# A fused RWKV-6 and MLP kernel: own terms of two rounds summed on TensorE, loads issued in program order, round 1 transposed within round 0, and twelve low words kept in the tiles of h

## The chip, the cores and the metric

The kernel runs on one core of one Trainium2 chip. The metric is the device time of one execution in microseconds. A core has five engines with an instruction queue each: TensorE (PE in the profile; its weight loads are PEld), VectorE (DVE), ScalarE (ACT), GpSimd (POOL) and SyncE (SP). In this kernel SP and ACT also issue the DMAs (SPq and ACTq in the profile). An engine works through its own queue in order, and waits on semaphores for the others.

## What is computed

The reference, cut to what matters. The inputs r, k, v, w are 4 x 8 x 768 x 48 (batch, head, time, channel), all float32; the two weights are 384 x 1536 and 1536 x 384, in float64 when they come in (the kernel reads them as pairs of 32-bit words).

```python
for t in range(S):                                   # attention, per batch and head
    cur = einsum(u * k[t], v[t])                     # the "own term" of step t
    y[t] = einsum(r[t], state + cur)
    state = w[t][:, None] * state + einsum(k[t], v[t])
x = y as (B, S, H*D)                                 # 4 x 768 x 384
xn = (x - mean) / sqrt(var + 1e-06) * g_ln
out = x + maximum(xn @ w_ch1, 0) @ w_ch2
```

## The kernel before, in words

**Rounds and units.** The work is cut into 8 rounds (4 batches x 2 halves of 384 time steps), and a round into 2 units of 4 heads. Units are numbered 0 to 15, two to a round. For each unit four loads of 72 KB each bring in w, k and r (one DMA per head, `load`, L120) into `nat_w`, `nat_k`, `nat_r`, which are double: a unit's number mod 2 chooses the buffer. v is loaded by four DMAs (`load_v`), and a second copy `vx` of the odd heads with its two halves of partitions exchanged comes from memory by four DMAs more (`load_vx`).

**Attention.** `turned` transposes w, k, r of one pair of heads on TensorE (three transposes), and ACT copies the PSUM tile out to wT, kT, rT. There are two PSUM buffers for this (`ps_t`). Then follow six levels. In a level, `quads` makes 24 small products per unit on TensorE (a_ps), `grow` multiplies rT and kT in place by the decays on DVE, and `keep` puts the products under a mask into A on DVE. `quads` of a level reads what `grow` of the level before has written, and `grow` of the level may not overwrite it before `quads` has read it, so that TensorE and DVE take turns. The decays' products come from `totals`. Behind the last level come `ends` (transposes of kT into kn), `states` (kv on TensorE, the states s on DVE), `exchanged` (ACT), `outputs` (y on TensorE, x on DVE). The own term is `take` (two products and a sum of 128 x 576 on DVE or POOL, which read `nat_k` and `nat_r` and the broadcast `u_bc`) and `own_term` (the sum times v).

**MLP.** `mlp` is a generator with 24 steps of three large matmuls each: 12 for h (one PSUM tile of 384 columns each, ReLU on ACT) and 12 for the output (o_ps). `fill(until, tasks)` spreads the tasks of a level evenly among the MLP steps that are due by then. From round 1 on, each level (here: slot, six to a round) is one call of it.

**Weights.** The weights come as 24 parts of 128 x 384 values (384 KB each as raw words). `fetch` loads a part into one of four `raw` buffers, `begin` makes three ACT instructions of it (one to w_sb, two to `rest`, the low words) and then fetches the part four ahead, and `join` makes three DVE instructions that put both together. `rest` has four buffers, so `begin` of a part waits for `join` of the part four before it. `converted` sees that a step of the MLP comes after the joins of its parts.

**What sets the order.** `InOrder` (L39) wraps PE, ACT, DVE and POOL, so that their instructions stand in the queue in the order of the program. SP was not wrapped: a scheduler placed its DMAs. All records of wrapped engines have line L49, that of the wrapper, and are told apart by tiles.

**Round 0** (L609 to L677) is written out by hand: transposes of units 0 and 1, six levels with idle matmuls between (`warm`), half of unit 2's and 3's transposes, the outputs, the layer norm, and the first weight parts. With L677 the MLP of round 0 begins.

Of the kernel before, what the change touches and what calls it, by code (L numbers as in the profile page):

```python
# [52 lines left out]
def kernel(  # L53
# [13 lines left out]
    PE, ACT, DVE, POOL = (  # L67
        InOrder(tc, e) for e in (nc.tensor, nc.scalar, nc.vector, nc.gpsimd)
# [22 lines left out]
    assert D <= HP and U == 2 and S % RN == 0 and DM % P == 0 and DF % P == 0  # L91
# [6 lines left out]
    p6 = ctx.enter_context(tc.tile_pool(name="p6", bufs=6))  # L98
    ph = ctx.enter_context(tc.tile_pool(name="ph", bufs=12))
# [20 lines left out]
    def load(q, which="wkr", eng=SP):  # L120
        for nm in which:
            for j in range(NH):
                eng.dma_start(
                    out=nat[nm][q % 2][:, ts(j // 2, TT), j % 2, 0:D],
                    in_=steps({"w": w, "k": k, "r": r}[nm], q, j),
                )

    def load_v(q):
        vn[q] = p4.tile([P, NH, TT, D], F32, tag="v", name=f"v{q}")
        for j in range(NH):  # L130
            SP.dma_start(out=vn[q][:, j], in_=steps(v, q, j))  # L131

    def load_vx(q):

        vx[q] = p4.tile([P, NP, TT, D], F32, tag="vx", name=f"vx{q}")
        for pr in range(NP):
            src = steps(v, q, 2 * pr + 1)
            for i in range(2):
                SP.dma_start(out=vx[q][ds(C * (1 - i), C), pr], in_=src[ds(C * i, C)])


    load(0, "wk")
    load(0, "r", ACT)
    load(1, "wk")
    u_bc = const.tile([P, H, D], F32, name="u_bc")
    ACT.dma_start(
        out=u_bc,
        in_=bass.AP(tensor=u.tensor, offset=u.offset, ap=[[0, P], [D, H], [1, D]]),
    )
# [3 lines left out]
    nought = const.tile([P, P], F32, name="nought")  # L153
    DVE.memset(nought, 0.0)
    eps = const.tile([P, 1], F32, name="eps")
# [6 lines left out]

    ident = const.tile([P, P], F32, name="ident")
    make_identity(nc, ident)
# [43 lines left out]
    def fetch(n=1, eng=ACT):  # L208
# [8 lines left out]
    def begin():  # L217
        nonlocal begun
        i = begun
        if i < len(parts):  # L220
            words = raw.pop(i)
            lo, hi = words[:, :, 0].bitcast(U32), words[:, :, 1].bitcast(F32)
            rest[i] = p4.tile([P, WC], I32, tag="rest", name=f"rest{i}")
# [30 lines left out]
    def warm(n):  # L254

        ps = ps_m.tile([P, RN], F32, tag="m", name="idle")
        for _ in range(n):
            PE.matmul(ps[:, 0:P], nought, nought, start=True, stop=True)
# [53 lines left out]
    def own_sums(q):  # L312
        o = st[q]["own"] = p2.tile([P, NH, TT], F32, tag="own", name=f"own{q}")
# [3 lines left out]
            axis=AX.X, op=ALU.add,  # L317
        )
# [179 lines left out]
    def norm(rnd):  # L498
# [6 lines left out]
        for i in range(TT):  # L505
            xn = p3.tile([P, H, D], F32, tag="xn", name=f"xn{rnd}_{i}")
# [18 lines left out]
    def mlp(rnd):  # L525
# [13 lines left out]
        for i in range(TT):  # L539
            ps = ps_m.tile([P, H, D], F32, tag="m", name=f"o_ps{name}_{i}")  # L540
            for f in range(FC):
                converted(len(parts) - FC + f + 1)
                PE.matmul(
                    ps.rearrange("p h d -> p (h d)"), hs[f][:, ts(i, P)], w2_sb[:, f, :],
                    start=f == 0, stop=f == FC - 1,
                )
                if f % KC == KC - 1 and f < FC - 1:
                    yield
            o = p2.tile([P, H, D], F32, tag="o", name=f"o{name}_{i}")
            DVE.tensor_tensor(out=o, in0=ps, in1=x[:, i], op=ALU.add)  # L550
            SP.dma_start(
                out=out[b, ds(f0 * RN + i * P, P), :].rearrange("t (h d) -> t h d", d=D), in_=o
            )
# [42 lines left out]
    pairs = range(NP)  # L596

    def take(eng, q):

        own_products(q, eng)  # L600
        own_sums(q)

# [8 lines left out]
    fetch(4, SP)  # L611
# [3 lines left out]
    take(DVE, u0)  # L615
    quads(u0, 0)
    load(new[0])
    for q in (u0, u1):
        load_v(q)
        load_vx(q)  # L620
    warm(2)
    grow(u0, 0)
    for nm in "wrk":
        run(each(turned, [u1], nm, pairs))
        warm(1)
    totals(0, DVE)
# [154 lines left out]
```

## Time and profile before

| what | value |
|---|---|
| runs | 636.33, 640.31, 642.42 us (median 640.31) |
| profiled execution, its own time | 638.57 us |
| its span, first to last instruction | 636.8 us, so 1.8 us lie around it |
| PE / DVE / ACT / POOL busy | 576.8 / 293.7 / 202.0 / 80.2 us |
| mean granted TensorE clock | 0.957 |
| DMA | 36.83 MB, 123250 packets, 116896 of them under 512 B |

How to read it: "busy" sums the durations of instructions; matmuls are pipelined, so that the start of the next row says more than the length of one. In a row of the timeline stand its start, its length, engine and line, the operation, output<-input, shapes, the number of instructions merged, and in brackets how long the engine stood idle before it and what released it. An h step is 3 matmuls and stands as 6 records.

### The profile page before, as it was taken

The page shows a single profiled execution, that of the slowest core. Times are in us where ns is not written, and L with a number is a line of the kernel's source. Part 1 is how long each engine was busy: PE and PEld are TensorE (multiplying, and loading weights), DVE is VectorE, ACT ScalarE, POOL GpSimd, SP SyncE. Part 2 cuts the span into 40 slices and gives each one's busy share as a digit, 9 for nine tenths or more (in the row PEclk, how much of TensorE's full clock was granted, in tenths as well). Part 3 has the DMA queues.
Part 4 walks back from the last instruction along what each step waited for, and adds up shares of the span by engine and source line. Part 5 has one row for each costly group of instructions (what it writes and reads, how often), then busy time and mean ns, then how long its engine had stood idle before and what let it go on. Part 6 is the DMA issues. An engine that isn't in the chain of part 4 may idle for free.

```text
span 636.8 us, 19302 instructions
## 1 busy us (share of the span) xinstructions
PE 576.8 (91%) x8560; PEld 392.5 (62%) x8560; DVE 293.7 (46%) x700; ACT 202.0 (32%) x426; POOL 80.2 (13%) x109
## 2 busy tenths in 40 slices
PE   6990983758999999999999999999999999999997
PEld 6880752436666666666666766667666666666554
DVE  3991697467464626272445543634427261221000
ACT  2361565556124321342124311441242104311200
POOL 6000001051006000240006000700040000000000
PEclk8995688869899999999999999999999999999999
DMA  9755577340432223113302241202100000000000
GB/s 166 169 95 114 106 185 188 105 107 8 92 63 51 38 48 74 31 31 63 75 27 39 47 85 29 51 1 47 39 14 2 9 21 13 1 14 25 1 12 25
DMA packets 123250, 36.83 MB, mean 58 GB/s; under 512 B 116896, under 2 KB 120096, under 8 KB 123168
## 3 DMA queue, kind: packets, MB, share of 16 engines
q1 hardware_dynamic: 116544, 26.96, 20.9%
q10 hardware_dynamic: 6624, 8.65, 5.0%
q8 instruction: 67, 1.10, 0.7%
q14 instruction: 15, 0.12, 0.1%
HBM read 30.87 MB, written 4.72 MB: 56 GB/s over the span
## 4 chain that ended last, share of the span: by engine, by line
PE 83%; DVE 4%; SPq 4%; ACT 3%; issue 3%; DMA 2%; ACTq 1%; DVEq 0%
PE o_ps L49 29%; PE h_ps L49 28%; PE a_ps L49 11%; PE y L49 3%; PE r_ps L49 2%; PE k_ps L49 2%; PE kv L49 2%; PE kn_ps L49 2%; PE xT_ps L49 2%; PE w_ps L49 1%; ACT rest L49 1%; DVE w_sb L49 1%; PE idle L49 1%; SPq L131 1%; DMA nat_k<-in_k_dram 1%
## 5 line engine op out<-in xcount | busy, mean ns | idle before, releaser
L49 PE MATMUL h_ps<-xT,w_sb 128*128 128x384 f32 x576 | 200.9, 500 | 5.7 <-DVE w_sb L49 3.3
L49 PE MATMUL o_ps<-w_sb,h 128*128 128x384 f32 x576 | 197.6, 489 | 2.0 <-DVE w_sb L49 2.0
L49 PEld LDWEIGHTS h_ps<-xT,w_sb 128*128 128x128 f32 x576 | 108.9, 195 | 74.7 <-issue 4.7
L49 PEld LDWEIGHTS o_ps<-w_sb,h 128*128 128x128 f32 x576 | 105.0, 191 | 63.1 <-DVE w_sb L49 2.6
L49 PEld LDWEIGHTS a_ps<-rT,kT 48*64 48x64 f32 x4608 | 75.4, 137 | 16.1 <-issue 14.1
L49 PE MATMUL a_ps<-rT,kT 48*64 48x32 f32 x4608 | 80.5, 221 | 4.4 <-issue 4.1
L49 ACT ACTIVATE h<-h_ps 128x384 f32<-128x384 f32 x96 | 46.4, 490 | 120.1 <-PE h_ps L49 115.7
L49 DVE TENSOR_TENSOR o<-o_ps,x 128x384 f32<-128x384 f32 x24 | 13.4, 557 | 136.6 <-PE o_ps L49 136.6
L49 DVE COPY_PREDICATED A<-mask,a_ps 128x384 f32<-128x384 int8 x80 | 54.5, 751 | 0.0
L49 POOL TENSOR_TENSOR vo<-v,own 128x576 f32<-128x576 f32 x12 | 13.9, 1156 | 308.0 <-DVE own L49 308.0
L49 DVE TENSOR_TENSOR rT<-rT,tot 128x384 f32<-128x384 f32 x80 | 43.7, 555 | 11.5 <-PE a_ps L49 11.5
L49 DVE TENSOR_TENSOR kT<-kT,tot 128x384 f32<-128x384 f32 x80 | 44.3, 554 | 8.3 <-PE a_ps L49 7.5
L49 DVE SCALAR_TENSOR_TENSOR s<-s,decay,kv 128x48 f32<-128x48 f32 x160 | 29.4, 258 | 35.3 <-PE kv L49 35.3
L49 DVE TENSOR_TENSOR x<-y,vo 128x288 f32<-128x288 f32 x32 | 13.2, 452 | 60.0 <-PE y L49 60.0
L49 PE MATMUL k_ps<-ident,nat_k 128*128 128x128 f32 x96 | 16.7, 302 | 20.5 <-DMA nat_w<-in_w_dram 16.5
L49 ACT ACTIVATE xT<-xT_ps,g_sb 128x384 f32<-128x384 f32 x24 | 13.8, 580 | 64.8 <-PE xT_ps L49 64.7
L49 ACT ACTIVATE rest<-raw 128x384 int32<-128x384 uint32 (+1 forms) x48 | 28.5, 594 | 4.4 <-DVE w_sb L49 3.7
L49 ACT COPY kT<-k_ps 128x384 f32<-128x384 f32 x32 | 14.7, 479 | 46.8 <-PE k_ps L49 46.4
L49 ACT COPY rT<-r_ps 128x384 f32<-128x384 f32 x32 | 14.8, 480 | 45.9 <-PE r_ps L49 45.9
L49 PEld LDWEIGHTS k_ps<-ident,nat_k 128*128 128x128 f32 x96 | 12.6, 155 | 25.8 <-ACT wT L49 17.2
L49 POOL TENSOR_TENSOR rk<-nat_k,nat_r 128x576 f32<-128x576 f32 x12 | 17.0, 1416 | 85.2 <-DVE own L49 84.8
L49 PE MATMUL r_ps<-ident,nat_r 128*128 128x128 f32 x96 | 17.1, 307 | 11.7 <-ACT rT L49 7.4
(63 smaller groups left out, 577.8 us busy)
## 6 DMA issues: line engine op xcount, KB each, us to landing
raw<-in_moe_w_ch_dram ACTq DMA_DIRECT2D x20, 384.0 KB, 3.3
nat_w<-in_w_dram SPq DMA_DIRECT2D x64, 72.0 KB, 2.4
nat_k<-in_k_dram SPq DMA_DIRECT2D x64, 72.0 KB, 2.4
v<-in_v_dram SPq DMA_DIRECT2D x64, 72.0 KB, 2.7
out_dram<-o SPq DMA_DIRECT2D x24, 192.0 KB, 1.9
nat_r<-in_r_dram SPq DMA_DIRECT2D x56, 72.0 KB, 2.4
vx<-in_v_dram SPq DMA_DIRECT2D x64, 36.0 KB, 2.2
raw<-in_moe_w_ch_dram SPq DMA_DIRECT2D x4, 384.0 KB, 4.8
```

What stands on the lines that cost most here:

```text
L49: return lambda *args, **kw: self.tc.keep_in_program_order(f(*args, **kw))
L131: SP.dma_start(out=vn[q][:, j], in_=steps(v, q, j))
```

## The change

1. **SP in program order.** `SPO = InOrder(nc.sync)`. All loads of round 0, the loads for units 4 and 5 in round 1, and every fetch of a weight part are issued by it (the weight parts' loads were ACT's from the fifth part on). r of unit 1 moves from ACT's queue to SP's.
2. **Own terms of units 0 to 3 on TensorE** (`own_by_pe`): two DVE products of 128 x 384 per unit from rT and kT, six matmuls of two columns with a tile `sel` that holds u in the columns of the two heads of a pair, and one ACT copy of 12 columns. `u_bc` is loaded only in round 1.
3. **vx from vn**: two DMAs per unit, SBUF to SBUF, in place of four from memory.
4. **Round 1 turned within round 0**: all twelve groups of transposes of units 2 and 3 stand between levels 1 to 4, where three groups of unit 2 stood at levels 3 and 4.
5. **Low words in the tiles of h**: `rest` of parts 0 to 11 uses the twelve buffers of h, and begin of these waits for no join; parts 12 to 23 have four buffers. Five parts are begun within the levels of round 0 where one was; eight by the start of the MLP where five were.
6. **The order after round 0**: `UNTIL` sets the MLP steps due by each slot: 16 at the end of round 1 (13 before), 33 at the end of round 2 (28 before), 48 at slot 16, near the end of round 3, in both, and the same from there. Round 1 has 3, 3, 3, 4, 4, 4 joins in its six slots and 3, 3, 3, 3, 4, 0 begins (before: 3, 2, 2, 3, 3, 4, 4 of both, in seven). In round 2 the states of both old units come in slot 0, outputs and layer norm in slot 1, `take` of units 4 and 5 in slot 2. `totals` of rounds 0, 1 and 2 stand on DVE behind the first `grow`. In round 0's MLP the first two output tiles are summed side by side.
7. **Small**: idle matmuls read a broadcast column of zeros.

The core of the diff:

```diff
+    PE, ACT, DVE, POOL, SPO = (
+        InOrder(tc, e) for e in (nc.tensor, nc.scalar, nc.vector, nc.gpsimd, nc.sync)
...
+        for i in range(2):
+            eng.dma_start(
+                out=vx[q][ds(C * (1 - i), C)].rearrange("p r c d -> p r (c d)"),
+                in_=vn[q][ds(C * i, C)]
+                .rearrange("p (r j) c d -> p r j (c d)", j=2)[:, :, 1],
+            )
...
-    load(0, "wk")
+    load(0, "w", SPO)
     load(0, "r", ACT)
-    load(1, "wk")
-    u_bc = const.tile([P, H, D], F32, name="u_bc")
-    ACT.dma_start(
...
-    load(1, "r", ACT)
+    load(0, "k", SPO)
+    load(1, "wrk", SPO)
+
+    sel = const.tile([P, H // 2, 2], F32, name="sel")
+    POOL.memset(sel, 0.0)
+    for j in range(2):
+        ACT.dma_start(
+            out=sel[ds(HP * j, D), :, j], in_=u.rearrange("(r j) d -> j d r", j=2)[j]
+        )
...
+    held = [ph.tile([P, RN], F32, tag="h", name=f"held{i}") for i in range(FC)]
+    LOW = 4
+
+    def fetch(n=1, eng=SPO):
...
-        if i < len(parts):
+        if i < len(parts) and i - joined < (len(held) if i < len(held) + LOW else LOW):
...
+            if i < len(held):
+                rest[i] = held[i].bitcast(I32)
+            else:
+                rest[i] = low.tile([P, WC], I32, tag="rest", name=f"rest{i}")
...
+    def own_by_pe(q):
+        b, f, g = units[q]
+        a = st[q]
+        ps = ps_t.tile([P, RN], F32, tag="t", name=f"own_ps{q}")
+        for pr in pairs:
+            rk = p3.tile([P, RN], F32, tag="xn", name=f"rk{q}_{pr}")
+            DVE.tensor_tensor(
+                out=rk, in0=a["r"][:, ts(pr, RN)], in1=a["k"][:, ts(pr, RN)], op=ALU.mult
+            )
+            for c in range(TT):
+                PE.matmul(
+                    ps[:, ts(pr * TT + c, 2)], rk[:, ts(c, P)], sel[:, NP * g + pr],
+                    start=True, stop=True,
+                )
...
-    take(DVE, u0)
     quads(u0, 0)
-    load(new[0])
-    for q in (u0, u1):
-        load_v(q)
-        load_vx(q)
-    warm(2)
+    own_by_pe(u0)
+    load(new[0], eng=SPO)
     grow(u0, 0)
...
+    own_by_pe(u1)
+    load(new[1], eng=SPO)
+    run(each(load_v, [u0, u1], [SPO]))
+    begin()
+    begin()
...
-    ahead = each(turned, new[:1], "wkr", pairs)
+    ahead = [t for q in new for t in each(turned, [q], "wkr", pairs)]
...
+        if lev < NLEV - 1:
+            run(ahead[(0, 2, 5, 8)[lev - 1] : (2, 5, 8, 12)[lev - 1]])
+            if lev != 3:
+                begin()
+            if lev == 2:
+                run(each(load_vx, [u0, u1], [SPO]))
...
-    run(each(turned, new[1:], "wkr", pairs))
...
+    UNTIL = [3, 6, 8, 11, 14, 16, 19, 21, 24]
...
+    JOINS, BEGINS = (3, 3, 3, 4, 4, 4), (3, 3, 3, 3, 4, 0)
```

**SP's queue, round 0, loads of units 2 and 3** (nat_w0 is the buffer of even units, nat_w1 of odd ones; v0 is unit 0's, raw4 the fifth weight part). Before:

```order
L212 DMA raw3_192<-in_moe_w_ch1_dram 128x768
L123 DMA nat_w0_85<-in_w_dram 128x3x48 x4
L123 DMA nat_k0_87<-in_k_dram 128x3x48 x4
L123 DMA nat_r0_89<-in_r_dram 128x3x48 x4
L131 DMA v0_278<-in_v_dram 128x3x48 x4
...
L123 DMA nat_w1_86<-in_w_dram 128x3x48 x4
L131 DMA v2_1337<-in_v_dram 128x3x48
L123 DMA nat_w0_85<-in_w_dram 128x3x48 x4
...
L123 DMA nat_k1_88<-in_k_dram 128x3x48 x4
L123 DMA nat_r1_90<-in_r_dram 128x3x48 x4
```

and in the changed kernel:

```order
L49 DMA raw3_210<-in_moe_w_ch1_dram 128x768
L49 DMA nat_w0_88<-in_w_dram 128x3x48 x4
L49 DMA nat_k0_90<-in_k_dram 128x3x48 x4
L49 DMA nat_r0_92<-in_r_dram 128x3x48 x4
L49 DMA nat_w1_89<-in_w_dram 128x3x48 x4
L49 DMA nat_k1_91<-in_k_dram 128x3x48 x4
L49 DMA nat_r1_93<-in_r_dram 128x3x48 x4
L49 DMA v0_393<-in_v_dram 128x3x48 x4
L49 DMA v1_398<-in_v_dram 128x3x48 x4
L49 DMA raw4_406<-in_moe_w_ch1_dram 128x768
...
L49 DMA vx0_576<-v0_393 64x2x144 x2
```

Unit 3's k and r moved up from behind the loads of v of round 1 and of w of unit 4; the fifth weight part, which ACT issued, now stands behind v of units 0 and 1, and vx behind four weight parts.

**ACT's queue, end of round 0's levels** (rT3 is unit 3's, kn0 unit 0's). Before:

```order
L49 COPY kT2_572<-k_ps2_1_635 128x384
L49 COPY rT2_640<-r_ps2_0_641 128x384
L49 COPY rT2_640<-r_ps2_1_646 128x384
L49 COPY kn0_718<-kn_ps0_0_719 128x384
L49 COPY kn0_718<-kn_ps0_1_724 128x384
L49 COPY A0_136<-a_ps0_5_659 32x12x32 x4
```

and in the changed kernel:

```order
L49 COPY rT3_724<-r_ps3_0_725 128x384
L49 COPY rT3_724<-r_ps3_1_730 128x384
L49 ACTIVATE w1_sb_181<-raw4_406 128x384
L49 ACTIVATE held4_187<-raw4_406 128x384 x2
L49 COPY kn0_807<-kn_ps0_0_808 128x384
L49 COPY kn0_807<-kn_ps0_1_813 128x384
L49 COPY kn1_818<-kn_ps1_0_819 128x384
L49 COPY kn1_818<-kn_ps1_1_824 128x384
L49 COPY own2_840<-own_ps2_829 128x2x3x2
```

The begin of the fifth part now stands ahead of the copies of kn, which the states wait for.

**ACT's queue, slot 0 and 1 of round 1** (h0_0_1 is the second h tile of round 0's MLP). Before:

```order
L49 ACTIVATE h0_0_0_1145<-h_ps0_0_0_1141 128x384
L49 ACTIVATE w1_sb_175<-raw6_981 128x384
L49 ACTIVATE rest6_1150<-raw6_981 128x384 x2
L49 DMA raw10_1154<-in_moe_w_ch1_dram 128x768
L49 ACTIVATE w1_sb_175<-raw7_1102 128x384
L49 ACTIVATE rest7_1159<-raw7_1102 128x384 x2
L49 DMA raw11_1163<-in_moe_w_ch1_dram 128x768
L49 ACTIVATE h0_0_1_1169<-h_ps0_0_1_1165 128x384
```

and in the changed kernel:

```order
L49 ACTIVATE h0_0_0_1201<-h_ps0_0_0_1197 128x384
L49 ACTIVATE w1_sb_181<-raw8_738 128x384
L49 ACTIVATE held8_191<-raw8_738 128x384 x2
L49 ACTIVATE w1_sb_181<-raw9_958 128x384
L49 ACTIVATE held9_192<-raw9_958 128x384 x2
L49 ACTIVATE h0_0_1_1220<-h_ps0_0_1_1216 128x384
L49 ACTIVATE w1_sb_181<-raw10_1015 128x384
L49 ACTIVATE held10_193<-raw10_1015 128x384 x2
```

The begins are two parts further ahead, write to `held`, and issue no DMA.

More of the change, by code (lines that the diff above doesn't have):

```diff
@@ L643 @@
         keep(0, lev)
-    run(each(ends, [u0], pairs))
-    finish(4)
-    run(each(ends, [u1], pairs))
-    warm(2)
-    finish(4)
-    take(DVE, u1)
-    load(new[1])
+    run(each(ends, [u0, u1], pairs))
+    for q in new:
+        own_by_pe(q)
+    finish(6)
     states(u0)
     exchanged(u0)
+    finish(2)
     warm(3)
@@ L664 @@
     moments(0)
-    begin()
-    run(each(turned, new[1:], "wkr", pairs))
+    load(units_of(2)[1], "w", SPO)
     for q in new:
@@ L669 @@
     norm(0)
+    begin()
+    join()
     warm(2)
@@ L699 @@
             if now:
+                if rnd <= 2 and lev == 0:
+                    totals(rnd, DVE)
                 keep(rnd, lev)
```

200 lines of the change are left out of this document (111 added, 89 removed).

## The prediction

> **What bounds the kernel now.** I read the kernel by stages first. In the table of windows each row has a stretch, then the busy time of PE, its weight loads, DVE, ACT and POOL, the granted TensorE clock, DMA share and GB/s.
>
> ```profile
> span 636.8 us, 19302 instructions
> core 0: us, PE busy (x) PEld busy (x) DVE busy (x) ACT busy (x) POOL busy (x), PEclk, DMA share, GB/s
> 0.00:48.00 48.00, 41.40 (x1018) 37.14 (x1019) 35.44 (x82) 19.77 (x42) 9.78 (x37) 0.96 0.74 143
> 48.00:65.00 17.00, 0.47 (x5) 0.23 (x3) 2.18 (x8) 2.19 (x5) 0.00 (x0) 0.58 0.58 116
> 65.00:74.00 9.00, 8.97 (x122) 7.71 (x123) 5.08 (x12) 3.56 (x8) 0.00 (x0) 0.50 0.58 118
> 74.00:140.00 66.00, 42.68 (x590) 27.56 (x589) 51.24 (x100) 41.93 (x82) 8.62 (x7) 0.84 0.59 145
> 140.00:203.50 63.50, 59.30 (x1093) 40.96 (x1092) 33.75 (x85) 24.44 (x53) 13.34 (x15) 0.95 0.28 56
> 203.50:637.00 433.50, 424.03 (x5755) 278.90 (x5746) 166.05 (x415) 110.08 (x238) 48.50 (x52) 1.00 0.14 32
> ```
>
> From 203.5 on TensorE is busy 98% at the full clock: the rest of the time is its work, and only fewer matmuls would shorten it. The losses lie ahead. From 48 to 65 all engines stand, from 65 to 74 TensorE runs at half the clock, and from 74 to 140, where the weights are converted beside round 1, it is busy 65% and DVE 78%. The waits of PE, summed by releaser, say why:
>
> ```profile
> PE k_ps L49 <- DMA nat_w<-in_w_dram: 16.5, 1, 16.5
> PE r_ps L49 <- ACT rT L49: 7.4, 2, 7.2
> PE w_ps L49 <- ACT wT L49: 7.0, 2, 6.8
> PE k_ps L49 <- ACT kT L49: 3.7, 1, 3.7
> PE h_ps L49 <- DVE w_sb L49: 3.3, 1, 3.3
> ```
>
> The first is unit 3's k. It was put down to nat_w, but the timelines of SP and PE show k and r issued at 52 to 56, behind eight DMAs of v, six of vx and w of unit 4, while w came at 36.93:
>
> ```profile
> 16.54 4.54 SPq L123 DMA_DIRECT2D nat_k<-in_k_dram  x4
> 21.13 3.36 SPq L123 DMA_DIRECT2D nat_r<-in_r_dram  x4
> 24.53 3.05 SPq L131 DMA_DIRECT2D v<-in_v_dram  x4
> 36.93 2.13 SPq L123 DMA_DIRECT2D nat_w<-in_w_dram  x4
> 52.00 2.25 SPq L123 DMA_DIRECT2D nat_k<-in_k_dram  x4
> 54.30 2.08 SPq L123 DMA_DIRECT2D nat_r<-in_r_dram  x4
> ...
> 64.95 1.54 PE L49 MATMUL k_ps<-ident,nat_k 128*128 128x128 f32 x6 [16.53 <-DMA nat_w<-in_w_dram]
> 73.84 4.37 PE L49 MATMUL h_ps<-xT,w_sb 128*128 128x384 f32 x12
> 203.32 1.57 PE L49 MATMUL a_ps<-rT,kT 48*64 48x32 f32 x96
> ```
>
> The others are transposes behind ACT: the copies that free the two PSUM tiles stand behind begins, and these behind joins (rest has four buffers).
>
> I split the time at three marks: the first h matmul (73.84), the first quads of round 3 (203.32), the end. The profiled execution took 638.57 us, 0.3% under the median of the runs, 640.31; the sum is made against 638.57.
>
> **Prices**, from the chain, ACT's and DVE's timelines, and the DMA issues (KB, us to landing):
>
> ```profile
> 88.13 1.53 PE a_ps L49 x96
> 145.97 0.89 PE kv L49 x48
> 162.59 1.54 PE y L49 x96
> 586.52 23.22 PE h_ps L49 x72
> ...
> 8.29 1.28 ACT L49 ACT_TABLE_LOAD   x1 [8.29 <-DMA nat_r<-in_r_dram]
> 9.69 0.84 ACT L49 COPY wT<-w_ps 128x384 f32<-128x384 f32 x2
> 37.11 0.86 ACT L49 COPY kn<-kn_ps 128x384 f32<-128x384 f32 x2 [2.47 <-PE kn_ps L49]
> 44.60 0.58 ACT L49 ACTIVATE w_sb<-raw 128x384 f32<-128x384 f32 x1
> 45.09 1.22 ACT L49 ACTIVATE rest<-raw 128x384 int32<-128x384 uint32 x2
> ...
> 72.62 0.95 DVE L49 TENSOR_TENSOR tot<-wT 128x768 f32<-128x768 f32 x1
> 75.24 0.56 DVE L49 TENSOR_TENSOR rT<-rT,wT 128x384 f32<-128x384 f32 x1
> 77.11 1.90 DVE L49 COPY_PREDICATED A<-mask,a_ps 128x384 f32<-128x384 int8 x2
> 78.79 0.80 DVE L49 TENSOR_SCALAR w_sb<-w_sb 128x384 f32<-128x384 f32 x2
> 80.20 0.75 DVE L49 TENSOR_SCALAR w_sb<-w_sb 128x384 f32<-128x384 f32 x2
> 93.33 1.03 DVE L49 COPY_PREDICATED A<-mask,a_ps 128x384 f32<-128x384 int8 x2
> 94.26 0.75 DVE L49 TENSOR_TENSOR rk<-nat_k,nat_r 128x576 f32<-128x576 f32 x1
> ...
> raw<-in_moe_w_ch_dram ACTq DMA_DIRECT2D x20, 384.0 KB, 3.3
> raw<-in_moe_w_ch_dram SPq DMA_DIRECT2D x4, 384.0 KB, 4.8
> ```
>
> An MLP step is 23.22/12 = 1.94 us; quads of both units 1.53; a unit's kv 0.89, its y 1.54. By starts on DVE: totals 2.6 (72.62 to 75.24), the four grows of a level 1.9 (to 77.11), keep 1.7 (to 78.79) or 0.9 (93.33 to 94.26), a join 1.4 (78.79 to 80.20), an operation of 128x576 0.75. A begin on ACT is 0.5 + 1.2 = 1.7, two copies 0.86. A unit's transposes take about 0.8 on TensorE, an estimate from those two copies, which keep pace with them.
>
> **Part 1: up to the first h matmul.** Without u_bc and r of unit 1 on ACT's queue (replaced by three tiny DMAs) its table load should come some 2 us sooner than 8.29 (five issues gone and two new, 0.5 each by 54.30, and the waits between them), and with it the first copy (9.69). That is lost again at once: totals (2.6 us) ran while DVE waited for unit 1 and now stands between unit 1's grow and level 0's keep. I count these as nil. Own terms cost DVE two products of at most 0.56 in place of three of 0.75, a gain under the transposes. Their six narrow matmuls have no row: at least a quads matmul's 1.53/96, at most a transpose's 0.8/6 each, 0.1 to 0.8 us a unit; near the lower end, as two columns stream. The twelve groups of transposes lie in TensorE's idle matmuls while DVE grows (1.9 us a level); three or four groups with ACT's copies fill that and no more.
>
> SP now issues k, r of unit 3 ahead of v, so the 16.5 us go. But what comes late next is the fifth weight part. Its issue stands behind w, k, r of unit 3 and v of units 0 and 1: 20 DMAs behind unit 2's r, which ended at 24.49; with unit 1's r on SP now and u_bc gone I put that at 25.2. At 0.56 us each (52.00) they take 11.2, at 0.76 (24.53) 15.2; the place is that of the slower row, but half-size vx loads no longer stand between, so 0.64: 12.8, raw4 issued near 38.5, landed 3.5 later (3.3 when alone, 4.8 in a pack) at 42. ACT stands at its begin until then, and behind it are the kn copies, which kv, states and y wait for: done with the begin at 43.7 instead of 37.11. From there to the end of y it was 10.5 (to 48.4, where PE's wait of 16.53 begins, less unit 3's w transposes, 0.8); with two kn copies more (0.86) and two own copies ahead of A it is about 11.8, so 55.5. Then x and moments (2.2, DVE's busy time from 48 to 65), norm and the turned x, about 3.3 (a third of the 8.9 from 64.95 to 73.84, the rest of which is k, r and quads at half the clock): first h near **61.0** (73.84). vx comes SBUF to SBUF, which no row shows: at least its 0.6 us of issue, at most a queued raw's 4.8; issued near 41, landed by 46, ahead of y at 52. By the two paces raw4 lands at 40.4 or 44.4 and the mark is 59.4 or 63.4; with no wait at all 54.4.
>
> [...] The nearest row is 2.08 for four; by it alone r of unit 1 would cost 2.1 where I took 0.7, and the result would be 601.4.
>
> **Part 2: round 1 with the weights.** By slot, DVE has 10.4 (grow 1.9, totals 2.6, keep 1.7, three joins 4.2), 7.8 (no totals), 7.0 (keep 0.9), 8.4 (four joins, 5.6), 9.2 (own term 0.75 too), 8.3 (no keep): 51.1. TensorE has 5.8 (three steps), 8.9 (quads 1.5, three steps, transposes of two units 1.6), 7.0 (two steps), 8.9, 7.3 (no transposes), 7.0 (two steps, kn 1.6): 44.9. ACT has at most four begins and a step's copies, 8.4. Since a slot's quads come behind the MLP steps of the slot before, and its grow behind the quads, each slot takes the larger: 10.4 + 8.9 + 7.0 + 8.9 + 9.2 + 8.3 = 52.7. Transposes of round 2 still stand behind pairs of begins (3.4 us) at w and r: I add 3, **55.7**. Begins no longer wait for joins up to part 11, and the raw loads run four parts ahead: 4.8 + 1.7 in flight over four buffers is 1.6 a part, under the 3.5 that 55.7/16 asks. By the same prices round 1 before has 50.8 on DVE (two takes at 2.25, fewer joins), and its stretch, 74 to 140, took 66, of which DVE was busy 51.2: 15 us of waits.
>
> **Part 3: round 2 to round 3's quads.** TensorE has 17 steps (33.0), six quads (9.2), kv 1.8, y 3.1, transposes 4.8 and 1.6, the turned x 1.3: 54.8; DVE had 33.75 in the 63.5 from 140. I add 3 for waits of y on PSUM and a clock not yet full: **57.8**.
>
> Round 3 then starts at 61.0 + 55.7 + 57.8 = 174.5, 28.8 sooner, with 33 steps done in place of 28: 5 x 1.94 = 9.7 less behind it, where TensorE sets the time (98% busy there). Summing two output tiles side by side, zeros as a broadcast and the other places of states, outputs and take in round 2 issue the same work; I give them nothing, as the first is PE's own order and the last lies beside 17 MLP steps; were it uncovered, take's two times 2.25 would be lost. 638.57 - 28.8 - 9.7 = **600.1**; I say 600.
>
> **Rivals.** *The wait for raw4 does not bite*: SP issues at 0.56 or less and the begin comes later than I think. First h at 54.4, 593.5. For it: a DMA share of 0.74 up to 48 leaves room; against: v took 0.76 a DMA there. *Conversion still stalls*: waits of transposes behind ACT persist, at 66/50.8 = 1.30 of DVE's sum: 66.4 for 55.7, 611. For it: still two PSUM tiles and begins ahead of copies; against: no begin waits for a join. *SP keeps a slow pace*, 1.13 a DMA as unit 2's k behind a pack of raws (16.54): raw4 10 us later, 610. For it: nothing is taken off SP here; against: the rows behind that one are faster.
>
> *Slower than before*: SP's strict order serializes the weights. Each raw waits at the head of SP for a begin, and holds up every load behind it. If only one part moves at a time, 4.8 + 1.7 + 1.4 + 0.5 = 8.4 us a part; sixteen parts from slot 0 take 134 instead of 55.7: 678. It decides from (55.7 + 38.5)/16 = 5.9 us a part. Against it: four buffers, and only 24 loads of 72 KB between these raws. *The change does not do what it says*: the standstill only moves from unit 3's k to raw4, and the gain is what is left of the first mark; that is the third rival.
>
> [...]
>
> **Chances.** Forecast 0.62, raw4 free 0.16, conversion stalls 0.13, SP slow 0.06, slower 0.03. The low end is 593.5 less most of the 6 of allowances, 589; the high end 611 plus the slower pace's 2.4, 613. A measurement of this kernel can tell about 1% from no change. Of the third rival I put 0.02 within 1%: faster 0.95, same 0.02, slower 0.03.
>
> **What would show it.** PE's 16.5 us wait gone; in its place ACT waiting 4 to 7 us for raw before the kn copies, and that begin near 42; first h near 61; round 1's waits of r_ps, w_ps, k_ps on ACT together under 6 us (18 before); quads of round 3 near 174; clock 0.95 or more from 74 to 140. It is wrong if the first h comes past 66, or if SP waits at raws while transposes wait for k or r.

## The result, and the profile after

The changed kernel took 618.51 us (median; 616.85 to 625.96) where the kernel before took 641.81 in the same comparison: a ratio of 0.968, 95% interval 0.962 to 0.975. It is faster, as forecast, but by 23 us where the forecast had 38.5 (638.57 to 600.1), and 5.5 us above the range of 589 to 613. The profiled execution, 625.96 us with a span of 624.0, is the longest of the changed kernel's; the others had spans of 615 to 621. So a stage that is read from its profile can look longer than it is in the median execution, and what a loss is worth is taken from the medians of the experiments. The windows of the profile, cut where the prediction cut before's:

```profile
0.00:48.00 48.00, 38.11 (x750) 34.05 (x750) 26.95 (x51) 21.60 (x47) 9.14 (x38) 0.88 0.76 160
48.00:65.00 17.00, 16.01 (x412) 14.98 (x411) 10.16 (x37) 9.16 (x21) 0.00 (x0) 0.74 0.30 69
65.00:74.00 9.00, 7.41 (x23) 4.56 (x24) 8.29 (x24) 5.63 (x12) 0.00 (x0) 0.81 0.86 180
74.00:140.00 66.00, 55.64 (x822) 36.08 (x820) 51.87 (x128) 39.48 (x84) 0.00 (x0) 0.92 0.48 121
140.00:203.50 63.50, 58.98 (x965) 39.91 (x965) 33.03 (x66) 16.63 (x38) 16.16 (x16) 0.84 0.35 72
203.50:624.00 420.50, 412.55 (x5622) 271.71 (x5620) 163.88 (x403) 106.68 (x231) 44.92 (x47) 1.00 0.15 33
```

The standstill from 48 to 65 is filled (PE 16.01 us, before 0.47), and 74 to 140 holds 13 us more of TensorE's work. But the granted clock is lower in the first and the fifth row than before (0.88 for 0.96, 0.84 for 0.95). PE's waits by releaser:

```profile
PE kn_ps L49 <- ACT kn L49: 7.2, 7, 5.5
PE r_ps L49 <- ACT rT L49: 4.6, 2, 4.3
PE a_ps L49 <- issue: 4.3, 4, 1.5
PE o_ps L49 <- DVE o L49: 2.5, 1, 2.5
```

The 16.5 us are gone; the first, second and fourth of these rows are what the experiments below take apart. The timelines around the first, of SP, ACT and PE:

```profile
34.91 4.80 SPq L49 DMA_DIRECT2D v<-in_v_dram  x8
39.81 2.99 SPq L49 DMA_DIRECT2D raw<-in_moe_w_ch_dram  x4
...
44.15 0.55 ACT L49 ACTIVATE w_sb<-raw 128x384 f32<-128x384 f32 x1 [6.26 <-DMA raw<-in_moe_w_ch_dram]
44.60 1.19 ACT L49 ACTIVATE held<-raw 128x384 int32<-128x384 uint32 x2
45.66 0.83 ACT L49 COPY kn<-kn_ps 128x384 f32<-128x384 f32 x2
...
47.64 5.28 PE L49 MATMUL own_ps<-sel,rk 128*128 128x2 f32 x24
52.84 1.53 PE L49 MATMUL kv<-v,kn 64*64 64x48 f32 x48
...
69.06 6.34 PE L49 MATMUL h_ps<-xT,w_sb 128*128 128x384 f32 x17
```

ACT stands 6.26 us for the fifth part, the copies of kn come behind it, and then 24 records of own matmuls (two to a matmul) hold TensorE for 5.28 us at half the clock before kv can start.

By the prediction's marks, from one profiled execution each (us; "first h" is the start of the first h matmul; the end of round 1 is taken at the first kv of round 2, which in the kernel before is 145.97, where the prediction cut at 140; "half" is the time at half the clock; "ratio" is that to before, a 95% interval):

| kernel | median | ratio | first h | to round 1's end (kv) | to round 3's quads | rest | half |
|---|---|---|---|---|---|---|---|
| before | 641.81 | | 73.84 | 72.1 | 57.4 | 433.5 | 54.6 |
| forecast | 600.0 | | 61.0 | 55.7 | 57.8 | 423.8 | |
| changed | 618.51 | 0.962 to 0.975 | 69.06 | 58.5 | 72.2 | 424.3 | 58.6 |
| e_order_only | 641.07 | 0.999 to 1.005 | 71.25 | 75.3 | 56.0 | 439.1 | 47.8 |
| e_order_fetch | 626.87 | 0.975 to 0.981 | 57.74 | 72.9 | 56.0 | 439.0 | 37.9 |
| u_fetch_act | 630.46 | 0.980 to 0.987 | 72.42 | 66.0 | 68.9 | 422.0 | 64.9 |
| d_own_dve | 616.94 | 0.961 to 0.968 | 62.15 | 57.3 | 65.5 | 425.3 | 30.7 |
| a_own_first | 619.02 | 0.962 to 0.970 | 68.50 | 58.1 | 69.2 | 422.4 | 51.2 |
| b_begin_late | 613.45 | 0.957 to 0.963 | 62.01 | 57.9 | 69.2 | 422.2 | 34.1 |
| c_mlp_between | 613.47 | 0.956 to 0.963 | 70.38 | 57.4 | 61.3 | 422.6 | 41.0 |
| g_mlp_ahead | 612.21 | 0.955 to 0.963 | 67.63 | 57.7 | 59.6 | 422.1 | 28.0 |
| bc | 610.23 | 0.948 to 0.957 | 62.16 | 57.5 | 64.0 | 423.7 | 34.1 |
| bcf | 602.17 | 0.933 to 0.943 | 61.69 | 52.3 | 62.6 | 423.8 | 23.9 |
| bcfo | 609.90 | 0.946 to 0.954 | 64.39 | 53.0 | 60.8 | 429.5 | 31.0 |
| bcf_wide | 600.03 | 0.934 to 0.942 | 60.90 | 51.9 | 61.0 | 424.0 | 14.5 |

The intervals leave out runs that lay over 1.5% above the fastest of their kernel: 624.28 of a_own_first, 610.45 and 610.99 of bcf, and three of the kernel before beside e_order_only, bc, bcf and bcfo.

The forecast's span was 598.2 and the profiled one is 624.0. The 25.8 us between them are 8.1 up to the first h, 2.8 in round 1, 14.4 in round 2 and 0.5 behind it. Of the signs that the prediction named, two came: the 16.5 us wait is gone, and ACT waits for the fifth part (6.26, forecast 4 to 7). The others did not: the first h is at 69.06, past the 66 that it named as being wrong; round 1's waits on ACT are 6.4 us (4.3, 1.8 and 0.3) and not under 6; round 3's quads are at 199.7 and not near 174; and the clock from 74 to 140 is 0.92 and not 0.95.

### The profile page after: what moved, and what is told of

It is laid out like the page before. It is cut to its first block, busy times and chain, and to the rows that moved or that the text cites. A ratio compares the mean times of both kernels' runs of the same rounds, so it can differ in the third digit from the quotient of the medians.

```text
span 624.0 us, 19313 instructions
## 1 busy us (share of the span) xinstructions
PE 588.7 (94%) x8588; PEld 401.3 (64%) x8588; DVE 294.2 (47%) x706; ACT 199.2 (32%) x430; POOL 70.2 (11%) x100
## 4 chain that ended last, share of the span: by engine, by line
PE 80%; DVE 8%; SPq 4%; ACT 3%; DMA 2%; issue 2%; ACTq 0%; DVEq 0%
PE o_ps L49 30%; PE h_ps L49 28%; PE a_ps L49 10%; SPq L49 4%; PE y L49 3%; DVE w_sb L49 3%; PE kv L49 2%; PE r_ps L49 2%; DMA raw<-in_moe_w_ch_dram 1%; PE kn_ps L49 1%; PE k_ps L49 1%; PE xT_ps L49 1%; PE w_ps L49 1%; ACT rest L49 1%; DVE A L49 1%
## 5 line engine op out<-in xcount | busy, mean ns | idle before, releaser
L49 PE MATMUL o_ps<-w_sb,h 128*128 128x384 f32 x576 | 205.5, 504 | 2.5 <-DVE o L49 2.5
L49 PE MATMUL h_ps<-xT,w_sb 128*128 128x384 f32 x576 | 198.4, 494 | 0.6 <-DVE w_sb L49 0.6
L49 PEld LDWEIGHTS o_ps<-w_sb,h 128*128 128x128 f32 x576 | 108.5, 197 | 68.3 <-issue 5.9
L49 PEld LDWEIGHTS h_ps<-xT,w_sb 128*128 128x128 f32 x576 | 106.8, 192 | 66.9 <-DVE w_sb L49 1.9
L49 PEld LDWEIGHTS a_ps<-rT,kT 48*64 48x64 f32 x4608 | 77.0, 140 | 19.3 <-issue 16.3
L49 ACT ACTIVATE xT<-xT_ps,g_sb 128x384 f32<-128x384 f32 x24 | 13.7, 580 | 70.5 <-PE xT_ps L49 70.4
L49 ACT COPY rT<-r_ps 128x384 f32<-128x384 f32 x32 | 14.4, 480 | 39.6 <-PE r_ps L49 39.5
L49 PEld LDWEIGHTS y<-v,A 64*64 64x64 f32 x384 | 20.8, 133 | 7.3 <-issue 6.0
L49 PE MATMUL kn_ps<-ident,kT 128*128 128x128 f32 x96 | 15.4, 289 | 9.0 <-ACT kn L49 7.2
L49 PE MATMUL y<-vx,A 64*64 64x48 f32 x384 | 23.8, 222 | 0.0
L49 PE MATMUL y<-v,A 64*64 64x48 f32 x384 | 23.8, 222 | 0.0
L49 ACT COPY kn<-kn_ps 128x384 f32<-128x384 f32 x32 | 14.4, 479 | 29.1 <-PE kn_ps L49 29.1
```

Of the source, the lines that this page charges most:

```text
L49: return lambda *args, **kw: self.tc.keep_in_program_order(f(*args, **kw))
```

## The experiments

**Where the gain comes from: e_order_only, e_order_fetch, u_fetch_act.** The first is the kernel before with the loads of units 2 and 3 ahead of v and vx, all in program order:

```diff
...
     quads(u1, 0)
+    take(DVE, u1)
+    load(new[1], eng=SPO)
+    for q in (u0, u1):
+        load_v(q, SPO)
+        load_vx(q, SPO)
...
-    take(DVE, u1)
-    load(new[1])
```

> The kernel before with one part of the change: the loads of units 2 and 3, then v and vx of units 0 and 1, issued by SP in program order, for which the own products of unit 1 on DVE move ahead of its level 0 keep. Weights, transposes of unit 3 and round 1's order stay as before. Theory (the 16.5 us wait for unit 3's k was the largest loss and this part alone removes it; the rest of the change gives the other 8 to 10 us): first h matmul at 58 to 61 instead of 73.84, time 624 to 628. Rival (with that wait gone the next loss takes its place, as round 1 is bound by the conversion of the weights, whose loads start no sooner): first h matmul near 60 but round 3's quads later than 194, time 630 to 635. Second rival (the other parts cost as much as they give): time 620 or less.

It gained nothing: 641.07, with the first h at 71.25. The theory falls, and so do both rivals, which had other times; the first rival also had the first h near 60. k and r of unit 3 were issued from 26.4 to 32.6, some 25 us sooner, and TensorE still stood 10 us ahead of k's transposes. ACT's and PE's timelines of e_order_only:

```profile
58.29 0.35 ACTq L49 DMA_DIRECT2D raw<-in_moe_w_ch_dram  x1
58.69 0.54 ACT L49 ACTIVATE w_sb<-raw 128x384 f32<-128x384 f32 x1 [7.16 <-DMA vx<-in_v_dram]
...
63.32 0.35 ACTq L49 DMA_DIRECT2D raw<-in_moe_w_ch_dram  x1
63.71 0.86 ACT L49 COPY wT<-w_ps 128x384 f32<-128x384 f32 x2 [3.38 <-DMA v<-in_v_dram]
...
64.24 1.54 PE L49 MATMUL k_ps<-ident,nat_k 128*128 128x128 f32 x6 [10.03 <-ACT wT L49]
```

ACT stood at the issue of a weight part's load until a load of vx, then one of v, had landed; the wT copy that frees the PSUM tile is behind it. The same rows stand in the kernel before, and the prediction does not use them:

```profile
59.49 0.54 ACT L49 ACTIVATE w_sb<-raw 128x384 f32<-128x384 f32 x1 [13.19 <-DMA nat_r<-in_r_dram]
...
64.42 0.86 ACT L49 COPY wT<-w_ps 128x384 f32<-128x384 f32 x2 [3.29 <-DMA v<-in_v_dram]
```

There, too, k_ps (64.95) starts when the first of the two wT copies (64.42, 0.48 each) is done: the 16.5 us ended with ACT, not with a load of k, the last of which was issued at 53.77 and landed 2.4 us later. The late loads had a part in it all the same: what let ACT go on at 59.49 was the landing of unit 3's r. In this trace ACT waits, ahead of the part's load issued at 59.10, for semaphore 100 until 59.02, where the r issued at 55.89 raises it, and the part's load uses 100 too; ahead of the load issued at 64.01 it waits for 108 until 63.62, where a v issued at 60.65 raises it, and the load at 64.01 uses 108. All 370 DMAs of the trace share eight semaphores. The next run adds, to e_order_only, the issue of all weight parts and of round 1's loads by SP:

```diff
-    def fetch(n=1, eng=ACT):
+    def fetch(n=1, eng=SPO):
```

> The kernel before with the loads in program order as in e_order_only, and in addition every load of a weight part, and the loads of round 1, issued by SP in program order instead of by ACT. Theory (the load order alone gained nothing because ACT, which issued the weight parts' loads, stood at those issues until older DMAs had landed, 7.2 and 3.4 us in e_order_only and 13.2 and 3.3 us before, with the copies of wT, kT and rT behind it; SP can stand there at no cost): these waits of ACT are gone, the first h matmul comes at 60 to 64 instead of 71.15, round 1's waits of TensorE for ACT shrink, time 622 to 630. Rival (round 1 is bound by the joins and the four buffers of the low words, wherever the loads are issued): first h near 62 but round 3's quads within 4 us of 203, time 634 to 640. Second rival (SP in strict order holds the weights up behind loads that wait for buffers): time 642 or more.

626.87, the theory's range; no wait of ACT at an issue is left, and the first h is at 57.74, sooner than forecast for the whole change and 11.3 us sooner than in the changed kernel. Its round 1 still takes 72.9, so the shorter round 1 (58.5) comes from the other parts. Then this one part undone in the changed kernel (the same line, the other way):

> The changed kernel with one part undone: the weight parts' loads from the fifth on are issued by ACT again; all else, the order of SP's loads too, stays. Theory (as above: ACT stands at the issue until an older DMA has landed, and everything behind it on ACT with it): ACT waits of 3 us or more at its load issues up to the first h matmul, which comes 3 to 8 us later than 69.06 or, if the fifth part lands sooner because its load no longer stands behind v, at about the same time with the waits moved to round 1; time 624 to 632. Rival (with the loads in program order nothing is pending that long, and ACT's issue is as good as SP's): time within 2 us of 618, or less, since the fifth part lands earlier.

630.46, 12 us of the gain lost, first h 3.4 us later. ACT again stands at its issues:

```profile
62.68 0.33 ACTq L49 DMA_DIRECT2D raw<-in_moe_w_ch_dram  x1
63.06 0.56 ACT L49 ACTIVATE w_sb<-raw 128x384 f32<-128x384 f32 x1 [3.04 <-DMA u_bc<-in_u_dram]
...
70.71 0.33 ACTq L49 DMA_DIRECT2D raw<-in_moe_w_ch_dram  x1
71.09 1.05 ACT L49 ACTIVATE xT<-xT_ps,g_sb 128x384 f32<-128x384 f32 x2 [4.11 <-DMA raw<-in_moe_w_ch_dram]
```

So the order of the loads alone gave nothing, and the order together with an issuing engine on which nothing waits gave 14 us. The issue by SP without the order was not run.

**What is lost up to the first h: d_own_dve, a_own_first, b_begin_late.** In d_own_dve, `take(DVE, q)` stands where `own_by_pe(q)` stood, and `u_bc` is loaded at the start.

> Part 2 of the change undone: the own terms of units 0 to 3 are products and sums on DVE at the same places in the program, from the untransposed k and r, and u comes as a broadcast at the start again; load order, early transposes and held low words stay. Theory (own terms on TensorE gain nothing near the start, since DVE's extra 3 x 0.75 us less 2 x 0.56 a unit is about 1.2 us, and cost 5.3 us for units 2 and 3 at half the clock): the first h matmul comes 1 to 4 us sooner, time 614 to 618. Rival (DVE is the bound between 10 and 41, and unit 3's k and r wait for the products that read the buffers of unit 1): each of the two takes ahead of level 1 delays the levels by its 2.26 us, the first h matmul comes 2 to 6 us later than 69.06, time 620 to 624. Second rival (the change's gain is chiefly this part): time over 628.

First h at 62.15, 6.9 us sooner, more than the theory's 1 to 4, and the median 616.94, in its range. Level 5's quads start at 37.1, in the changed kernel at 37.5, so units 0 and 1 gain nothing from TensorE by these profiles. But they set d_own_dve's fastest execution (612.0) against the changed kernel's longest; the medians differ by 1.6 us and the intervals overlap, so no difference in time is shown. That profile has no own matmuls and 6.8 us of half clock from 43.9 to 50.7 where the changed kernel's has 13.7 from 43.1, so it does not say which weighs more. In a_own_first the own matmuls of units 2 and 3 go ahead of `ends`:

> The own matmuls of units 2 and 3 go ahead of the transposes of kn, into the time in which TensorE waits for the kn copies. Theory (the 24 narrow matmuls, 5.3 us at 0.213 us each in the changed kernel's trace, stand between kn and kv on the path to the first h matmul): they now lie from about 41 to 46, kv starts near 49 instead of 52.84, the first h matmul comes 3.5 to 5 us sooner than 69.06, near 65, and the time is 613.5 to 615.5. Rival (they are covered: behind kv the path is set by vx, by the own copies or by ACT's copies of A and rx): the first h matmul stays within 1.5 us of 69.06 and the time near 618.

619.02 and first h at 68.50, by the numbers the rival; but its profiled execution had half the clock from 21.24 to 38.31, levels 1 to 4 ended 4 us later, ACT's wait for the part was 0.19 us by then, and own matmuls and kn followed each other in one row. It doesn't decide. In b_begin_late the begin at level 4 is dropped, and one more stands behind the states:

```diff
-            if lev != 3:
+            if lev < 3:
                 begin()
...
     own_term(u0, DVE)
     begin()
+    begin()
```

> The begin of the fifth weight part leaves level 4 of round 0 and stands, with the sixth, behind the states. Theory (ACT standing at that begin from 37.9 to 44.15 holds the kn copies, and TensorE, with nothing to do, falls to half the clock): the kn copies come at 40 to 42 instead of 45.66, the own matmuls at 0.11 to 0.15 us each instead of 0.213, the first h matmul near 61 to 63, 6 to 8 us sooner, and the time 611 to 613. Rival (the wait moves to the next arrival: vx, which is issued behind four weight parts that wait for begins, or the sixth part): the first h matmul gains under 2 us and y waits for a DMA. Second rival (the parts, begun later, are missed in round 1): the first h matmul near 62 but the end of round 1 back at 127, time 617 to 619.

First h at 62.01, as the theory had it, kn copied from 40.9, time 613.45, somewhat above its range and 5.1 us under the changed kernel's; no wait moved to vx. The own matmuls still took 3.3 us.

**What is lost in round 2: c_mlp_between, g_mlp_ahead.** PE in the changed kernel, slot 1 and 2 of round 2:

```profile
145.36 1.48 PE L49 MATMUL a_ps<-rT,kT 48*64 48x32 f32 x50 [1.41 <-issue]
146.77 4.21 PE L49 MATMUL o_ps<-w_sb,h 128*128 128x384 f32 x6
153.49 4.21 PE L49 MATMUL o_ps<-w_sb,h 128*128 128x384 f32 x6 [2.51 <-DVE o L49]
157.62 2.79 PE L49 MATMUL a_ps<-rT,kT 48*64 48x32 f32 x96
```

Two output tiles end at 151, both PSUM tiles of `ps_m` are full, and the third tile's first step waits for DVE to add x. From 145.54 to 166.02 the clock is half, and an MLP step takes 4.2 us (1.94 at the full clock). The clock changes of this profile lie whole multiples of 3.41 us apart (last section), and the windows are cut on that raster:

```profile
142.13:145.54 3.41, 2.00 (x139) 1.88 (x131) 1.44 (x4) 0.00 (x0) 0.00 (x0) 1.00 0.40 71
148.95:152.37 3.42, 2.02 (x4) 0.57 (x2) 3.02 (x10) 0.30 (x1) 0.00 (x0) 0.50 0.48 107
```

The half clock begins before the wait for o: the step ahead of it, with TensorE busy for 2.00 of 3.41 us, holds the gap of 1.41 within the quads, in which TensorE waits for nothing that the profile shows ("issue"). The wait for o falls into the half clock, in a step that is no busier. c_mlp_between:

```diff
                 for f, q in zip(due, old):
                     f(q)
+                    if lev == 1:
+                        mlp_step()
```

> In slot 1 of round 2 one step of the MLP stands behind y of unit 2 and one behind y of unit 3, where the steps due all followed the quads of units 4 and 5. Theory (the 288 small matmuls in a row from 140.25 to 146.84 with the gaps beside them bring the half clock of 145.54 to 166.02): that stretch is 10 us or less or gone, from the end of round 1 (kv of units 2 and 3) to the quads of round 3 it takes 60 to 66 us instead of 72.2 in the profiled execution, and the time is 613 to 617. Rival (the half clock comes from the gaps of 1.41 and 2.51 us, where o_ps waits for o on DVE, or falls there in some executions only): the stretch stays as long or comes and goes between executions, and the median stays within 2 us of 618.5.

61.3 for 72.2 and 613.47, the theory's numbers; the medians differ by 5.0 us. But it took the wait for o away as well, so it doesn't separate theory and rival. g_mlp_ahead does: one `mlp_step()` ahead of that loop, which completes the two tiles, and none within.

> The changed kernel with one step of the MLP, the one that completes the first two output tiles, ahead of both y's of slot 1 in round 2; both y's and the quads of units 4 and 5 stay in one piece (288 small matmuls). Theory A (what cost the time in slot 1 was TensorE's wait of 2.5 us for o and the gaps beside it, in the same 3.41 us as the small matmuls): the wait for o is gone, as in c_mlp_between, and so is the gain: round 2 60 to 63 us, time 612 to 615. Theory B (the small matmuls in one piece alone bring the half clock): the wait for o is gone, but a half-clock stretch of 7 us or more follows the quads, round 2 65 to 72 us, time 616 to 619.

Theory A's numbers: round 2 in 59.6, 612.21, which is 6.3 us under the changed kernel's median. Up to 100 us its half-clock stretches are those of the changed kernel to within 0.1 us, and from 108.0 to 606 there is none, with 288 small matmuls in a row:

```profile
143.08 1.02 PE L49 MATMUL a_ps<-rT,kT 48*64 48x32 f32 x56 [1.17 <-issue]
144.03 2.20 PE L49 MATMUL o_ps<-w_sb,h 128*128 128x384 f32 x6
146.16 1.92 PE L49 MATMUL a_ps<-rT,kT 48*64 48x32 f32 x96
```

My first theory, the run of small matmuls alone, falls: this run has it and keeps the clock. The wait for o is gone, and the gap within the quads is still there, 1.17 us. By the windows it lies across two steps of the clock, both busier than the changed kernel's one:

```profile
138.72:142.13 3.41, 3.19 (x220) 3.11 (x213) 1.81 (x5) 0.00 (x0) 0.00 (x0) 1.00 0.55 162
142.13:145.55 3.42, 2.47 (x61) 1.90 (x61) 2.19 (x6) 0.00 (x0) 0.00 (x0) 1.00 0.62 116
```

So what the two runs show is that an MLP step further ahead is worth 5 to 6 us, and that the 288 small matmuls alone didn't bring the half clock. What causes the gap, and whether its place against the clock's steps or the order decided here, stays open.

**Both together, and round 1: bc, bcf, bcfo.** bc is b_begin_late with c_mlp_between.

> The later begin of the fifth part and the MLP steps between the y's, together. Theory (two separate losses, one up to the first h matmul, one in round 2): their gains add, 5 + 5 us less than the changed kernel, first h near 62, round 3's quads near 182, time 607 to 610. Rival (the gain of the one is the clock's recovery that the other gives too): 612 to 614.

610.23, just above the theory's 607 to 610; the two gains alone would give 608.4. The second wait of the list was in slot 3 of round 1; ACT and PE of the changed kernel:

```profile
95.76 0.55 ACT L49 ACTIVATE w_sb<-raw 128x384 f32<-128x384 f32 x1
100.52 1.23 ACT L49 ACTIVATE rest<-raw 128x384 int32<-128x384 uint32 x2 [4.21 <-DVE w_sb L49]
...
105.88 1.54 PE L49 MATMUL r_ps<-ident,nat_r 128*128 128x128 f32 x6 [4.29 <-ACT rT L49]
```

bcf puts that slot's transposes ahead of its joins and begins:

```diff
-                tasks += each(turned, new, "wkr"[lev - first], pairs)
+                ahead = each(turned, new, "wkr"[lev - first], pairs)
+                tasks = ahead + tasks if (rnd, lev) == (1, 3) else tasks + ahead
```

> As the run before, and in slot 3 of round 1 the transposes of r of units 4 and 5 stand ahead of the slot's joins and begins. Theory (there ACT stands 4.2 us in the begin of part 16, whose low words have only four buffers and wait for the join of part 12, and TensorE waits 4.3 us behind it for rT, then runs 6.8 us at half the clock): that wait of TensorE falls under 1 us, round 1 takes 53 to 56 us instead of 58.5, time 3 to 5 us less than the run before, 603 to 606. Rival (DVE's joins bound this slot, h_ps then waits for w_sb instead): the wait moves to h_ps or a_ps and the time is within 1.5 us of the run before.

Round 1 in 52.3, and 602.17, 8 us less than bc where the theory had 3 to 5. In PE's timeline these transposes now come at 91.02 with a wait of 0.24:

```profile
91.02 0.93 PE L49 MATMUL r_ps<-ident,nat_r 128*128 128x128 f32 x6 [0.24 <-ACT rT L49]
91.78 5.97 PE L49 MATMUL h_ps<-xT,w_sb 128*128 128x384 f32 x18
```

bcfo takes the own terms of units 2 and 3 to POOL and DVE.

> As the run before, and the own terms of units 2 and 3 are two products each on POOL and a sum on DVE, no longer on TensorE. Theory (their 24 matmuls stand between kn and kv and take 3.3 us where the later begin already stands): the first h matmul 2.5 to 4 us sooner, near 58.5, time 2 to 4 us less than the run before, 600 to 603. Rival (behind kv the states, ACT's copies of A and rx and vx set the time): first h within 1 us of 61.8, time within 1.5 us of the run before. Second rival (POOL's products slow DVE's states, norm and joins beside them): first h later.

The theory falls, 609.90. Both rivals had a part: kv comes 3.1 us sooner (42.43), then y waits for vx, and beside POOL's products DVE's three xn take 3.46 us where bcf has 1.26. PE's wait in bcfo:

```profile
PE y L49 <- DMA vx<-v: 1.8, 1, 1.8
```

DVE's timeline in bcfo, and then in bcf:

```profile
59.04 3.46 DVE L49 TENSOR_SCALAR xn<-x,mv,rstd 128x384 f32<-128x384 f32 x3
```

```profile
58.98 1.26 DVE L49 TENSOR_SCALAR xn<-x,mv,rstd 128x384 f32<-128x384 f32 x3
```

Together with half the clock from 47.62 to 68.10 the first h comes 2.7 us later than in bcf. Most of the 7.7 us between the medians is not in this stretch: 5.7 us lie behind round 3's quads (429.5 for 423.8), where the edit changes nothing. There the profile has 5.5 us of a_ps's gaps that it puts down to nothing, bcf's 2.0, and 6.8 us of half clock, bcf's 3.4. Their cause stays open, so the time doesn't decide between the rivals.

**What an own matmul costs: bcf_wide.**

```diff
-                    ps[:, ts(pr * TT + c, 2)], rk[:, ts(c, P)], sel[:, NP * g + pr],
+                    ps[:, ts(pr * TT + c, HP)], rk[:, ts(c, P)],
+                    sel[:, None, NP * g + pr].broadcast_to([P, HP // 2, 2]),
```

> bcf with one size changed: each own matmul streams 64 columns (the two of u repeated 32 times) instead of 2, and the copy takes the first two of each 64. The weights loaded and the result are the same. Theory (in all traces so far the clock was halved in the 3.41 us after a stretch filled with own matmuls, though TensorE counts as 90% busy there, so matmuls of two columns count as idle for the clock): the half-clock stretches at 20 to 27 and 44 to 51 go, own matmuls take about 0.11 to 0.16 us each, first h at 57.5 to 60 instead of 61.6, time 598 to 601. Rival (the clock falls there because of the gaps around them, whatever streams): the stretches stay, and with 62 columns more the own matmuls take longer, first h at 62 to 64, time 603 to 605.

The stretches of half clock at 20 and 44 are gone, and 32 times the columns cost no time: in both kernels the matmuls start 0.11 us apart at full clock. PE's row of the own matmuls in bcf, then in bcf_wide:

```profile
42.33 3.25 PE L49 MATMUL own_ps<-sel,rk 128*128 128x2 f32 x24 [0.19 <-ACT kn L49]
45.51 1.53 PE L49 MATMUL kv<-v,kn 64*64 64x48 f32 x48
```

```profile
42.10 2.89 PE L49 MATMUL own_ps<-sel,rk 128*128 128x64 f32 x24 [0.19 <-ACT kn L49]
44.93 0.92 PE L49 MATMUL kv<-v,kn 64*64 64x48 f32 x48
```

The first h, 60.90, is later than the theory's 57.5 to 60; its profile has another stretch of half clock, from 57.66 to 64.48. At 600.03 it is the shortest here, but its interval is that of bcf: only the clock is shown to differ, not the time. Both beat the changed kernel by 16 to 18 us.

## Why the prediction was right in direction and wrong in size

- **The 16.5 us wait.** It went, but the step that reads it failed: it is put down to unit 3's k, and k had landed by 56.2, 8.7 us before the wait ended. ACT's standing at its own load issues (13.19 and 3.29 us) set the end. That the wait went all the same was luck: the change moves those issues too; by that reading e_order_only alone should have gained, and it gained nothing.
- **The wait for the fifth part.** Its mechanism was right: forecast at a begin of 42, measured 44.15, as v was issued until 39.71, where the prediction had the fifth part's own issue near 38.5. b_begin_late confirms it.
- **kn copies to the end of y, 11.8 us.** From 45.66 to 61.7 it took 16.0. The term that failed is the price of the own matmuls, "0.1 to 0.8 us a unit, near the lower end, as two columns stream". They cost 12 x 0.111 = 1.33 us a unit at full clock, beyond my upper bound, and 2.6 at half. The bound counted six matmuls at a transpose's price; but each is two records, as an h step's 3 matmuls are 6, and each record costs nearly that price (0.111 us against 0.8/6 = 0.133). The columns don't set it (0.11 with 2 in bcf and with 64 in bcf_wide). That the 128x128 weights do is my estimate, as loading them fills 2.8 of the 2.9 us there; no run changed their size. And I had not placed the own matmuls between kn and kv on TensorE.
- **The clock.** The sum has no term for a lower clock between the kn copies and the end of y; what it adds to that stretch is ACT's copies. TensorE set it: it ran from 47.64 to 61.7 without a gap, and the clock was half from 43.14 to 56.79.
- **Round 1, 55.7.** Measured 58.5. The sum by slots, 52.7, holds for bcf, which has no wait at part 16: 52.3. The 3 us that I added for waits were 5.8. I saw that low words of parts 12 on have four buffers, and did not follow begin 16 to the join of part 12, directly behind which it now stands: ACT waited 4.2 us for it, and TensorE 4.3 for ACT.
- **Round 2, 57.8.** Measured 72.2, the largest miss in the profile. The step that failed is the term put at nothing: "Summing two output tiles side by side" and "the other places of states, outputs and take", of which I said "I give them nothing". Both outputs and the quads now stand with no MLP step between, and two tiles at once leave no PSUM tile for the third: a wait of 2.5 us, and half clock from 145.54 to 166.02. One MLP step further ahead gives 59.6 in g_mlp_ahead's profile and 6.3 us in the median. Ahead of the half clock lies the gap of 1.41 us that the profile puts down to nothing; whether the gap began it stays open.
- **Behind round 3's quads, 423.8.** Measured 424.3: five more steps done, as forecast.
- **The rivals.** Conversion stalled chiefly once, and round 1 was 2.8 us longer than forecast where that rival had 10.7; SP issued the fifth part at 39.81, 1.3 us late, and its strict order serialized nothing. With the three places mended (bcf) the kernel takes 602, where the forecast was 600. That is in part luck: its first h is 0.7 us later than forecast, its round 1 3.4 shorter and its round 2 4.8 longer, and these cancel.

## What to carry to other kernels

When a long wait is put down to a load, look up when that load landed, and at the rows of the engine that frees the output tile: a load issue that waits is a wait for everything behind it on that engine (13.19 us of ACT in the kernel before), so issue loads from an engine with nothing else to do (14.2 us between the medians of e_order_only and e_order_fetch). Follow each new instruction to what stands behind it on its own engine, and each tile count to the first request that exceeds it. Price a short matmul by its records and not by its columns (here 0.111 us a record at full clock with 2 columns, 2.89 us for 24 with 64), and look behind a gap on TensorE for half clock as well (20.5 us of it behind the gap of 1.41 in the changed kernel).

## What the runs showed of the hardware

- **Stretches at half the clock are whole multiples of 3.41 us long here.** In the profile of before they last 3.42, 23.90, 3.41, 6.83, 3.42, 10.24 and 3.41 us, in the changed kernel's 6.82, 13.65, 3.42, 6.83, 3.41, 20.48 and 3.41, besides one that the span's end cuts: one to seven times 3.41. Within each of the two profiles their starts and ends lie on one raster of 3.413 us, which begins 2.8 us behind the first instruction in the profile of before and 2.2 in the changed kernel's. Executions of one kernel differ in their mean clock, and the time goes with it: the changed kernel's six are four with spans of 614.9 to 617.3 at 0.964 to 0.967 and two of 620.9 and 624.0 at 0.953. That the place of the raster makes this difference is not shown, as one execution of a kernel was traced.
- **TensorE's busy share in a step, and the clock of the next.** Over the profiles of before, of the changed kernel and of all experiments but bcf_wide I took the steps of 3.41 us at full clock, and the share of each in which TensorE was busy with other than own matmuls (and their weight loads). Of those over 0.8, all 1949 are followed by a step at full clock; of those under 0.4, all 34 by one at half; between, 48 of 144 by one at half. Before and the changed kernel alone have 302 of 302, 7 of 7 and 7 of 23. The changed kernel's step from 142.13 to 145.54, with the gap of 1.41 us and a share of 0.59, is one of the 7 between.
- **Half the clock behind own matmuls of two columns, and not of 64.** Ten steps in which TensorE was over 0.8 busy, own matmuls counted, were followed by one at half; without them each is under 0.8. In the changed kernel it is the step from 15.84 to 19.25: 0.81 with them, 0.50 without, and 6.82 us of half clock behind it. In bcf_wide, with 64 columns, a step of 0.87 (35 records of own matmuls and their weight loads in it) was followed by full clock.
- **POOL beside DVE**: the three xn on DVE took 3.46 us beside POOL's two products of 128x576, 1.41 and 1.40 us (bcfo), and 1.26 without them (bcf).
